# A scale chunk of a joint-attention block loaded through another engine's DMA queue

## The chip, the cores and the metric

The kernel runs on 1 core of one Trainium2 chip. The metric is the device time of one execution in microseconds; before the change it is 116.68 us, the median of 3 runs (116.31 to 116.77). A core has TensorE (matmuls, PE in the profile, its weight loads PEld), VectorE (DVE), ScalarE (ACT), GpSimd (POOL) and SyncE (SP). They run their own instruction streams and wait for each other through semaphores. Transfers between the chip's memory (HBM) and the on-chip memory are issued by SyncE, ScalarE or GpSimd, each into a queue of its own (q1, q10 and q0 in the profile), and 16 DMA engines carry them out.

## The reference

One block of a diffusion transformer with two streams, an image of 2 x 256 tokens and a text of 2 x 32 tokens, 1152 channels, all bf16. Each stream is normalized, scaled and shifted by vectors computed from a condition `c`, and projected to q, k and v; the streams attend jointly; each is projected out, gated and added to its input.

```python
mod_i = (_silu(c) @ wmod_img).reshape(B, 6, 1, D)
shi, sci, gai = (mod_i[:, 0].copy(), mod_i[:, 1].copy(), mod_i[:, 2].copy())
hi = _layernorm(x_img, axis=-1) * (1 + sci) + shi
qkvi = hi @ wqkv_img
...
q = jnp.concatenate([qt, qi], axis=1)
scores = jnp.einsum('bqd,bkd->bqk', q, k) * D ** (-0.5)
p = _softmax(scores, axis=-1)
a = jnp.einsum('bqk,bkd->bqd', p, v)
out_i = x_img + gai * (ai @ wo_img)
```

The change concerns `sci`, the scale of the image stream: columns 1152 to 2303 of `wmod_img`.

## The kernel before

The image stream is four tiles of 128 tokens (x tiles 0 to 3), tiles 0 and 1 of the first image, 2 and 3 of the second. The 1152 channels are nine blocks of 128. The order of instructions on each engine is written out by hand: an engine runs its instructions in the order in which the program names them, and a wait holds all that stands behind it on that engine. TensorE therefore works through the first stage in this order (L261 to L333):

- `warm` (L139): matmuls on zeros, 4, then the transpose of `c` for silu (L148), then 11 more; nothing uses their results.
- `mod_scale(0)` (L213): the scale of channel blocks 0 and 1. `mod_cols` (L207) multiplies 18 blocks of `w_sc_i` by silu(c) (L210); ScalarE adds 1 and writes `mod_i` (L221).
- `x_transposes(0)` (L187, L193): the nine blocks of the normalized tile 0, `xn_i`, are turned so that channels lie on partitions; one warming matmul; the same for tile 1.
- `v_block` with chunk 0 (L256, L250): the value projection of tiles 0 and 1 over the channel blocks 0 and 1, eight matmuls of 128x512.
- the transposes of tile 2, `mod_scale(1)`, the value projection of tile 2, and so on through tile 3 and the chunks 1 to 3, and then the query and key projections and the text stream.

ScalarE evacuates the transposes. Blocks 0 and 1 are scaled on the way (`evac_scaled`, L196 to L199), which needs `mod_i`; the others are copied (`evac_low` L202, `evac_high` L205) and scaled later in place (`apply_mod`, L223). Between these copies ScalarE takes the square root for the normalization (`std_of`, L175). VectorE makes the statistics (L168), the reciprocal (L179) and the normalized tile (`out_of`, L180) in the order tile 0, 1, then 2, with the first third of tile 3's statistics ahead of tile 2's normalization.

The scale weight `w_sc_i` and the value weight `w_v_i` are loaded in four chunks each of two channel blocks (the last of three), `KC` in the code. A scale chunk takes 256 columns of all 1152 rows, in pieces of 512 B. A value chunk takes 256 full rows of 1152 columns, in pieces of 2304 B, and an x tile 128 such rows.

All these loads stand on SyncE's queue in the order of L103 to L114: x tile 0, x tile 1, scale chunk 0, x tile 2, value chunk 0, x tile 3, then scale and value chunks in turn, and behind them the weights of the later stages. On ScalarE's queue stand three transfers ahead of ScalarE's first instruction: the condition `c` (L81, 4.5 KB), and two tiny reads (L84) of 16 rows and 2 columns into a tile `first`, one from the scale weight, one from the value weight. Nothing reads `first`.

The transfers issued by SyncE and ScalarE use eight completion semaphores in rotation: the ninth waits, ahead of its issue, for the landing of the first.

Of the kernel before, what the change touches and what calls it, by code (L numbers as in the profile page):

```python
# [14 lines left out]
def kernel(  # L15
# [14 lines left out]
    nc = tc.nc  # L30
    bf = mybir.dt.bfloat16
# [3 lines left out]
    B, NI, D = x_img.shape  # L35
    NT = x_txt.shape[1]
    P = 128
# [19 lines left out]
    small = ctx.enter_context(tc.tile_pool(name="small", bufs=4))  # L57
# [12 lines left out]
    def w_view(src):  # L70
        return src.rearrange("(kt p) n -> p kt n", p=P)
# [7 lines left out]

    c18 = small.tile([B * KT, P], bf, bufs=1)  # L80
    nc.scalar.dma_start(c18[:], c.rearrange("b (kt p) -> (b kt) p", p=P))  # L81
    first = small.tile([16, 2, 2], bf, bufs=1)
    for n, (src, c0) in enumerate(((wmod_img, D), (wqkv_img, 2 * D))):
        nc.scalar.dma_start(first[:, n, :], src[0:P:8, c0:c0 + 2])  # L84
    x_i = act.tile([P, NIT, D], bf)
    x_t = act.tile([P, D], bf)
    xf_full = act.tile([P, 2 * VC + 64], bf)
# [1 line left out]
    w_sc_i = wpool.tile([P, KT, D], bf, tag="w", name="w_sc_i")  # L89
    w_v_i = act.tile([P, KT, D], bf, tag="V", name="w_v_i")  # L90

    def load_x(i):
        nc.sync.dma_start(x_i[:, i, :], xi_t[:, i, :])  # L93

    def load_sc(ch):
        k0, k1 = KC[ch]
        nc.sync.dma_start(w_sc_i[:, :, k0 * P:k1 * P], w_view(wmod_img)[:, :, D + k0 * P:D + k1 * P])

    def load_v(ch):
        k0, k1 = KC[ch]  # L100
        nc.sync.dma_start(w_v_i[:, k0:k1, :], w_view(wqkv_img)[:, k0:k1, 2 * D:3 * D])

    load_x(0)  # L103
    load_x(1)
    load_sc(0)
    load_x(2)
    load_v(0)
    load_x(3)
    for ch in range(1, len(KC)):
        load_sc(ch)  # L110
        if ch < len(KC) - 1:
            load_v(ch)
# [786 lines left out]
```

## Time and profile before

| what | value |
|---|---|
| median of 3 runs | 116.68 us |
| profiled execution, its own time | 116.51 us |
| its span | 114.5 us |
| TensorE busy | 108.8 us (95%) |
| VectorE, ScalarE, GpSimd busy | 75.0, 39.7, 27.6 us |
| read from HBM | 39.36 MB |
| mean rate over the span | 357 GB/s |
| SyncE's queue q1 | 39.64 MB, 90.9% of 16 engines |
| ScalarE's queue q10 | 0.18 MB, 0.6% |

The span is the time from the first to the last instruction that the profile shows; the execution's own time has what lies around it too. TensorE's idle time falls into the first 10 us and the last 3 us. The rates of the first slices are lower than later: of 40 slices of 2.86 us, the first eight moved 81, 315, 346, 355, 372, 383, 398 and 411 GB/s.

In lines of the timeline and the chain, the first number is the start in us from the span's start, the second the length; what stands in square brackets is how long the engine was idle ahead of it and who ended the wait. "SPq" is SyncE's issue of a transfer; the transfer itself goes on after it. In the list of DMA issues the last number is the time from issue to landing.

### The profile page before, as it was taken

Reading aid. Unit: us, or ns where it says so; the run is one execution under the profiler, and the core shown is the slowest. Engines: PE = TensorE matmul, PEld = TensorE weight load, DVE = VectorE, ACT = ScalarE, POOL = GpSimd, SP = SyncE. Lnnn points to the kernel's source line nnn. Section 1 sums busy time; section 2 is a strip of 40 time slices with the busy share of each in tenths; the row PEclk is TensorE's granted clock in tenths of the full one; section 3 lists DMA queues with packets and bytes.
Section 4 is the critical chain, followed back from the end, with each engine's and each line's share of the span. In section 5 each row is a group of like instructions: output and inputs, shape, how many; then the busy total and the mean of one; then the engine's idle time right before and its main releaser. Section 6 shows DMA issues by size and latency. Waiting matters only on the chain.

```text
span 114.5 us, 2919 instructions
## 1 busy us (share of the span) xinstructions
PE 108.8 (95%) x1230; PEld 64.7 (56%) x1230; DVE 75.0 (66%) x150; ACT 39.7 (35%) x93; POOL 27.6 (24%) x60
## 2 busy tenths in 40 slices
PE   5978999999999999999999999999999999999990
PEld 1344564544954444444447658787697566567560
DVE  1698920353399999999999760227656803998770
ACT  2729760342380630730009924025646700001000
POOL 7000103550050000000000051501540560899200
PEclk9999999999999999999999999999999999999999
DMA  3999999999999999999999999999999999962042
GB/s 81 315 346 355 372 383 398 411 412 411 408 407 412 405 416 401 412 412 411 412 411 411 410 405 411 404 389 399 411 408 403 409 410 398 388 273 102 26 163 69
DMA packets 22775, 40.87 MB, mean 357 GB/s; under 512 B 1311, under 2 KB 6571, under 8 KB 22763
## 3 DMA queue, kind: packets, MB, share of 16 engines
q1 hardware_dynamic: 21680, 39.64, 90.9%
q0 software_dynamic: 608, 0.88, 2.1%
q10 hardware_dynamic: 475, 0.18, 0.6%
q8 instruction: 9, 0.15, 0.5%
q14 instruction: 3, 0.02, 0.1%
HBM read 39.36 MB, written 1.34 MB: 356 GB/s over the span
## 4 chain that ended last, share of the span: by engine, by line
PE 87%; DMA 6%; SPq 2%; DVE 1%; issue 0%
PE qkps L486 31%; PE ps L821 16%; PE va L250 11%; DMA x_i<-in_x_img_dram 6%; PE aps L729 5%; PE ps L552 4%; PE sps L585 4%; PE gps L374 3%; PE ops L839 2%; PE ps L350 2%; PE ps L401 2%; PE ps L660 2%; SPq L93 1%; PE mps L210 1%; PE gps L794 1%; PE tp L193 1%
## 5 line engine op out<-in xcount | busy, mean ns | idle before, releaser
L486 PE MATMUL qkps<-hT_i,t 128*128 128x512 bf16 x162 | 35.6, 379 | 0.0
L486 PEld LDWEIGHTS <-t 128*128 128x128 bf16 x162 | 15.6, 98 | 18.3 <-issue 0.2
L448 DVE SCALAR_TENSOR_TENSOR sacc<-w_v_i,mod_img,sacc 128x1152 f32<-128x1152 bf16 x16 | 22.7, 1418 | 0.5
L821 PE MATMUL ps<-t,aT 128*128 128x384 bf16 x99 | 16.4, 326 | 0.0
L250 PE MATMUL va<-w_v_i,hT_i 128*128 128x512 bf16 x63 | 14.6, 379 | 0.5 <-DMA w_v_i<-in_wqkv_img_dram 0.5
L821 PEld LDWEIGHTS <-aT 128*128 128x128 bf16 x117 | 11.0, 98 | 6.8 <-issue 0.5
L827 DVE TENSOR_TENSOR tmp<-ps,gb 128x384 bf16<-128x384 f32 x11 | 6.1, 551 | 6.1 <-DMA gb<-mod_scratch 4.9
L250 PEld LDWEIGHTS <-hT_i 128*128 128x128 bf16 x63 | 5.8, 97 | 7.2 <-ACT hT_i L198 0.8
L805 POOL TENSOR_TENSOR w_og<-t,gb 128x384 bf16<-128x384 bf16 x9 | 8.8, 1006 | 4.5 <-PE ps L821 4.5
L507 POOL TENSOR_SCALAR svn<-svr 128x128 bf16<-128x128 bf16 x1 | 0.3, 298 | 32.8 <-ACT svr L156 32.8
L168 DVE BATCH_NORM_STATS2 stats<-x_i 128x6 f32<-128x384 bf16 x12 | 5.9, 543 | 2.9 <-DMA x_i<-in_x_img_dram 2.9
L436 ACT ACTIVATE qT<-qkps 128x512 bf16<-128x512 f32 x9 | 4.9, 596 | 6.4 <-PE qkps L486 6.4
L452 ACT CAST shi<-sacc 128x1152 bf16<-128x1152 f32 x2 | 2.3, 1152 | 13.7 <-DVE sacc L448 13.7
L142 PE MATMUL wps<-wz 128*128 128x512 bf16 x16 | 5.6, 499 | 1.2 <-DVE wz L127 1.2
L234 POOL TENSOR_SCALAR hT_i<-hT_i,mod_img 128x256 bf16<-128x256 bf16 x5 | 2.5, 510 | 15.9 <-ACT rstd L175 9.2
L742 DVE TENSOR_SCALAR aT<-aps,sv 128x288 bf16<-128x288 f32 (+2 forms) x11 | 4.3, 457 | 1.9 <-PE aps L729 1.9
L552 PEld LDWEIGHTS <-t 128*128 128x128 bf16 x162 | 4.9, 98 | 0.7 <-issue 0.5
L156 DVE CAST kT<-qkps 128x512 bf16<-128x512 f32 x3 | 2.1, 686 | 4.7 <-PE qkps L486 4.7
L552 PE MATMUL ps<-hT_t,t 128*128 128x64 bf16 x162 | 5.0, 193 | 0.0
L828 DVE TENSOR_TENSOR o<-tmp,x_i 128x384 bf16<-128x384 bf16 x11 | 4.7, 428 | 0.4
L744 ACT ACTIVATE aT<-aps,sv 128x288 bf16<-128x288 f32 (+2 forms) x11 | 4.0, 468 | 2.2 <-PE aps L729 2.2
L729 PE MATMUL aps<-pT,v_i 128*128 128x288 bf16 (+2 forms) x44 | 4.8, 264 | 0.0
(166 smaller groups left out, 148.0 us busy)
## 6 DMA issues: line engine op xcount, KB each, us to landing
t<-in_wmod_txt_dram SPq DMA_DIRECT2D x3, 2592.0 KB, 21.9
t<-in_wqkv_img_dram SPq DMA_DIRECT2D x6, 864.0 KB, 13.1
t<-in_wqkv_txt_dram SPq DMA_DIRECT2D x2, 2592.0 KB, 18.4
t<-in_wmod_img_dram SPq DMA_DIRECT2D x3, 864.0 KB, 11.6
w_home<-in_wmod_img_dram SPq DMA_DIRECT2D x1, 2592.0 KB, 14.7
t<-in_wqkv_txt_dram SPq DMA_DIRECT2D x3, 864.0 KB, 14.2
t<-in_wo_img_dram SPq DMA_DIRECT2D x1, 2592.0 KB, 17.8
t<-in_wo_txt_dram SPq DMA_DIRECT2D x3, 864.0 KB, 15.6
```

The source lines that it names most:

```text
L142: nc.tensor.matmul(ps[:], lhsT=wz[:, 0:P], rhs=wz[:], start=True, stop=True)
L168: nc.vector.bn_stats(stats[0:np_, k, :], x_ap[:, k * CH:(k + 1) * CH])
L250: nc.tensor.matmul(ps[:], lhsT=hT_i[:, kt, i * P:(i + 1) * P], rhs=w_v_i[:, kt, half * VW:(half + 1) * VW], start=(kt == 0), stop=(kt == K ...
L436: nc.scalar.mul(out_ap, in_ap, SCALE)
L448: nc.vector.scalar_tensor_tensor(saccs[b][:], w_v_i[:, kt, :], ap, saccs[b][:], op0=ALU.mult, op1=ALU.add)
L486: nc.tensor.matmul(pss[j - j0][:], lhsT=wq[:, kt, j * P:(j + 1) * P], rhs=hT_i[:, kt, :], start=(kt == 0), stop=(kt == KT - 1))
L552: nc.tensor.matmul(ps[:, j - j0, :], lhsT=wq[:, kt, j * P:(j + 1) * P], rhs=hT_t[:, kt, :], start=(kt == 0), stop=(kt == KT - 1))
L729: nc.tensor.matmul(bank[:, off:off + c1 - c0], lhsT=lhsT, rhs=rhs, start=(first[id(bank)] == n), stop=(final[id(bank)] == n))
L805: nc.gpsimd.tensor_mul(w_og[:, dt, 0:CH], w_o_i[:, dt, NG0:D], gb[:, B - 1, NG0:D])
L821: nc.tensor.matmul(ps[:, 0:cw], lhsT=aT[:, dt, t0:t0 + P], rhs=rhs, start=(dt == DTS[0]), stop=(dt == DTS[-1]))
L827: nc.vector.tensor_mul(tmp[:, 0:cw], ps[:, 0:cw], gb[:, b, cs])
L828: nc.vector.tensor_add(o[:, cs], tmp[:, 0:cw], x_i[:, i, cs])
```

## The change

Scale chunk 0 is issued by ScalarE, behind `c` and the remaining tiny read of the value weight, and no longer by SyncE between x tiles 1 and 2. The tiny read of the scale weight is left out. The other scale chunks stay on SyncE's queue. No computation changes.

```diff
     c18 = small.tile([B * KT, P], bf, bufs=1)
     nc.scalar.dma_start(c18[:], c.rearrange("b (kt p) -> (b kt) p", p=P))
-    first = small.tile([16, 2, 2], bf, bufs=1)
-    for n, (src, c0) in enumerate(((wmod_img, D), (wqkv_img, 2 * D))):
-        nc.scalar.dma_start(first[:, n, :], src[0:P:8, c0:c0 + 2])
+    first = small.tile([16, 2], bf, bufs=1)
+    nc.scalar.dma_start(first[:], wqkv_img[0:P:8, 2 * D:2 * D + 2])
...
-    def load_sc(ch):
+    def load_sc(ch, queue=nc.sync):
         k0, k1 = KC[ch]
-        nc.sync.dma_start(w_sc_i[:, :, k0 * P:k1 * P], w_view(wmod_img)[:, :, D + k0 * P:D + k1 * P])
+        queue.dma_start(w_sc_i[:, :, k0 * P:k1 * P], w_view(wmod_img)[:, :, D + k0 * P:D + k1 * P])
...
+    load_sc(0, nc.scalar)
     load_x(0)
     load_x(1)
-    load_sc(0)
     load_x(2)
     load_v(0)
     load_x(3)
```

## The prediction

> **What bounds the kernel now.** I read the chain that ended last, in order of time, then the timeline of the first 25 us, then the DMA issues and queues of short stretches, last two tables by stretch. The chain (start, length, what):
>
> ```profile
> 2.99 0.43 SPq L101
> 3.42 0.04 issue
> 3.47 6.89 DMA x_i<-in_x_img_dram
> 10.36 0.02 issue
> 10.38 0.56 DVE stats L168
> ...
> 11.68 0.68 PE tp L193 x9
> ...
> 22.18 4.48 PE va L250 x20
> ```
>
> From 11.68 us TensorE runs almost without a break to 111.36 us, through stages that the change does not touch. What delays TensorE at 11.68 is therefore paid at the end, less the small waits before 22 us. The timeline shows what stands ahead of that point:
>
> ```profile
> 7.21 0.58 DVE L180 TENSOR_SCALAR xn_i<-x_i,mv,rstd 128x1152 bf16<-128x1152 bf16 x1
> ...
> 7.30 0.61 PE L210 MATMUL mps<-sT,w_sc_i 128*128 128x2 bf16 x18 [0.79 <-DMA w_sc_i<-in_wmod_img_dram]
> ...
> 8.58 0.67 PE L193 MATMUL tp<-ident,xn_i 128*128 128x128 bf16 x9
> ...
> 9.72 1.89 PE L250 MATMUL va<-w_v_i,hT_i 128*128 128x512 bf16 x8 [0.48 <-DMA w_v_i<-in_wqkv_img_dram]
> ...
> 10.17 0.29 ACT L175 ACTIVATE rstd<-mv,eps_t 128x1 f32<-128x1 f32 x1
> ...
> 20.06 0.91 PEld L210 LDWEIGHTS <-w_sc_i 128*128 128x128 bf16 x27 [0.15 <-DMA w_sc_i<-in_wmod_img_dram]
> ```
>
> TensorE waits for the first scale chunk until 7.30. The normalized tile 0 is ready at 7.21 + 0.58 = 7.79, and the transposes behind the scale matmuls start at 7.85. A chunk that came earlier could win 0.05 us there; one that comes later holds everything behind it on TensorE.
>
> **What a later chunk costs.** Call M the start of the scale matmuls, 7.30 now. The second set of transposes ends at 8.58 + 0.67 = 9.25, that is M + 1.95, and only then can the first value matmuls (L250) run; now they wait 0.48 more for the value weights. Eight of them take 1.89: M + 3.84. Beside them ScalarE makes rstd of x tile 2 behind evacuations that need the chunk, done at 10.46 = M + 3.16; VectorE adds a reciprocal (0.15) and the normalization (0.58), M + 3.89, and the third transposes follow some 0.05 later, M + 3.94. They start at 11.68 now. Of a shift there, the 0.15 us wait at 20.06 gives back 0.15. So the time changes by **M + 3.94 - 11.68 - 0.15 = M - 7.89**. Up to M = 7.89 that is nothing: a chunk 0.59 us later only eats the 0.48 us wait for the value weights, VectorE's wait for x tile 3 (landed at 10.36) and the 0.15 us.
>
> **The change, part by part.** *ScalarE's queue.* The transfer of 0.1 KB that goes took 0.33 us to issue, the chunk 0.43 on SyncE: ScalarE is free at 2.3 in place of 2.2. Its table loads, silu and second table load follow, the last ending at 5.0 against 5.58, when rstd of tile 0 needs it: 0 on the path, with 0.5 of cover. SyncE's slowest early issue of a small transfer, 0.82 (L93 at 2.12), would use 0.4 of that cover; its blocked one, 2.76 (L101 at 4.64), would make tile 0 late by about 0.7, still ahead of a late chunk. I take 0.
>
> *SyncE's queue.* The chunk's issue and the gap behind it, 0.43 + 0.04, go; x tile 2, value chunk 0 and x tile 3 are each issued 0.47 us sooner. They land 6.1, 6.7 and 6.9 us after their issue, and the DMA engines are at a share of 1.02 to 1.16 in every half microsecond from 3.0 to 6.0: they queue for the engines, not for the issue. Worth between 0 and 0.47; I take 0. SyncE also waits 0.2 us at 4.4 for the tiny transfer (waits of SyncE's queue); the next issue is blocked until 7.40 anyway, so 0.
>
> *No tiny read of the scale weight.* No row prices what it does for the chunk. Low 0. High, by the stretch where the engines were slowest once running, 239 GB/s over 5.5 to 6.5 against 302 before it: 63 KB, 0.2 us. I take 0.
>
> *The chunk itself, 576 KB in rows of 512 B.* This decides. In order on one queue it followed x tiles 0 and 1. These are the landings:
>
> ```profile
> w_sc_i<-in_wmod_img_dram SPq DMA_DIRECT2D x1, 576.0 KB, 5.6
> ...
> x_i<-in_x_img_dram SPq DMA_DIRECT2D x1, 288.0 KB, 6.1
> first<-in_wqkv_img_dram ACTq DMA_DIRECT2D x1, 0.1 KB, 4.4
> ...
> w_v_i<-in_wqkv_img_dram SPq DMA_DIRECT2D x1, 576.0 KB, 6.7
> ```
>
> With the issues at 1.65, 2.12, 1.76 and 2.99 they land at 7.25, 8.2, 6.2 and 9.7. After the change the chunk is issued behind c and the other tiny transfer, about 1.76, still at its old time; but SyncE issues x tile 2 at 1.65 and value chunk 0 at about 2.1. It now shares the engines with transfers that used to follow it. How are two queues shared? The queue rows of 94 to 96 us, GpSimd's beside SyncE's:
>
> ```profile
> q0 software_dynamic: 133, 0.54, 65.5%
> q1 hardware_dynamic: 134, 0.30, 38.2%
> ```
>
> 133 packets against 134, though the one kind carries 4 KB and the other 2.2: a turn each by packets, not by bytes. The chunk is 9 x 128 = 1152 packets of 512 B, the x tiles and value chunk 128 to 256 of 2304 B, so turn by turn it loses. Against it stands the 0.1 KB transfer: alone on ScalarE's queue, it landed 4.4 us after its issue, 1.1 us before the chunk that was issued ahead of it on the other queue, where c, on an idle chip, was there 2.3 us after its issue. That is nearer to arrival order than to turns. Low end: arrival order, the chunk behind x tile 2 alone, M = 8.2. High end: turns throughout; some 36 packets of SyncE's on each engine (x tile 2, value chunk 0, x tile 3, the rest of tile 1) go first, so half of the chunk is still to come when x tile 3 lands at 10.36, shared with the next 512 B chunk: 2 x 288 KB at 302 GB/s is 1.9 us, M = 12.3. Between them: the first part in arrival order, the rest in turns with value chunk 0. Then x tiles 0 to 2, the chunk and value chunk 0 all go before its last packet, the same bytes that stood before the value chunk's landing now: **M = 9.72**. I take this, since both rows then hold for their part. Below the low end, with the chunk served even before x tile 1, M would be about 6.3, but tile 1 and with it both normalizations would come later: no gain there.
>
> Sum: 9.72 - 7.89 = +1.83 us. On the profiled execution's 116.51 us (span 114.5) that is 118.34; the median of the runs is 0.17 above it: **118.5 us**.
>
> [...]
>
> **Rivals.** *Turns throughout.* For it the 133 to 134, against it the 4.4 us. M between 10.4 and 12.3, say 11.3: +3.4, 120.1 us.
>
> *Arrival order, behind x tile 2 only.* For and against the other way round. M = 8.2: +0.3, 117.0 us.
>
> *Not slower: two queues fill the engines' gap.* In 5.5 to 6.5 us they moved 239 GB/s; if the chunk's packets ran while another queue's first reads were slow, value chunk 0 and x tile 3 would land up to 0.2 us sooner and the chunk by 7.3: 116.68 - 0.3 = 116.4 us. It decides only where M stays under 7.89, which needs the chunk to get ahead of x tile 2, issued 0.1 us before it. "The transfer is hidden anyway" ends here too, at 116.7.
>
> *The clock falls.* Between 6.51 (last warming matmul) and M TensorE would do nothing for 3.2 us. After its last matmul of all, at 111.36, the granted clock fell at about 114, 2.7 us later:
>
> ```profile
> 111.40:114.00 2.60, 0.00 (x0) 0.00 (x0) 0.28 (x1) 0.00 (x0) 0.00 (x0) 1.00 0.26 76
> 114.00:114.40 0.40, 0.00 (x0) 0.00 (x0) 0.00 (x0) 0.00 (x0) 0.00 (x0) 0.55 0.00 0
> ```
>
> At the start matmuls of 512 columns follow at 427 ns until 4.84 and at 216 after, 3.6 us from the first one at 1.23. A second such stretch at half speed costs 1.8 us on top of the forecast: 120.3 us. Against it: the pause may not last long enough. [...]
>
> **Chances.** Forecast 0.40; turns throughout 0.16; arrival order 0.18; not slower 0.13; the clock falls 0.13. A measurement of this kernel can tell about 0.5%, 0.58 us, from no change. The forecast and the two of 120 us are slower by more: 0.69; of arrival order, a landing a little later adds 0.03. Same: 0.15 of arrival order and 0.08 of not slower. Faster: the remaining 0.05. The range runs from 116.6 (0.1 left out below) to 120.3 (0.1 above); the forecast's own, M from 9.1 to 10.4, is 117.9 to 119.2.
>
> **What would show it.** Right: the scale matmuls (L210) start at about 9.7 with some 3 us of waiting for w_sc_i, the value matmuls about 11.7 with no wait for w_v_i, the third transposes at 13.6, and the wait at 20.06 gone. The share rule shows in the packets of ScalarE's queue beside SyncE's between 4 and 9 us. Wrong: scale matmuls at or before 7.9; then the chunk was not held up, and the sum falls to 0 or below. L250 at 427 ns apart after 10 us would be the clock.

## The result

The changed kernel takes 122.08 us, the median of 6 executions (121.22 to 123.88); the kernel before, run beside it, 116.65 us (116.31 to 117.09). The ratio is 1.0448, 95% interval 1.0417 to 1.048: slower by about 5.2 us. (The two medians lie 5.4 us apart; the ratio leaves out the execution of 123.88 us, in which the granted clock was lowest, 0.958.) The profiled execution took 122.23 us with a span of 120.2 us, 5.7 more than before. The change moved some code, so L209 is what L210 was, L192 was L193, L249 was L250.

The chain that ended last, in order of time, now hangs on the chunk itself:

```profile
1.77 9.46 DMA w_sc_i<-in_wmod_img_dram
11.28 0.64 PE mps L209 x18
11.91 0.98 PE tp L192 x9
...
17.70 0.52 PE tp L192 x9
```

The chunk is issued at 1.77, as expected, and landed only after 9.46 us. The DMA issues of short stretches give the others (x tile 2, the chunk, value chunk 0, x tile 3):

```profile
x_i<-in_x_img_dram SPq DMA_DIRECT2D x1, 288.0 KB, 4.5
...
w_sc_i<-in_wmod_img_dram ACTq DMA_DIRECT2D x1, 576.0 KB, 9.5
...
w_v_i<-in_wqkv_img_dram SPq DMA_DIRECT2D x1, 576.0 KB, 7.5
...
x_i<-in_x_img_dram SPq DMA_DIRECT2D x1, 288.0 KB, 7.9
```

With the issues at 1.64, 1.77, 2.12 and 2.60, x tile 2 landed at 6.1, value chunk 0 at 9.6 and x tile 3 at 10.5: all ahead of the chunk. The last two are no earlier than before. In the timeline:

```profile
3.17 4.60 PE L141 MATMUL wps<-wz 128*128 128x512 bf16 x11
...
7.15 0.58 DVE L179 TENSOR_SCALAR xn_i<-x_i,mv,rstd 128x1152 bf16<-128x1152 bf16 x1
...
11.28 0.64 PE L209 MATMUL mps<-sT,w_sc_i 128*128 128x2 bf16 x18 [3.51 <-DMA w_sc_i<-in_wmod_img_dram]
...
13.12 1.17 PE L192 MATMUL tp<-ident,xn_i 128*128 128x128 bf16 x9
...
14.93 2.77 PE L249 MATMUL va<-w_v_i,hT_i 128*128 128x512 bf16 x6 [0.22 <-ACT hT_i L197]
...
17.49 0.72 PE L192 MATMUL tp<-ident,xn_i 128*128 128x128 bf16 x9
```

The normalization is where it was (7.15 against 7.21) and waits. M, the start of the scale matmuls, is 11.28 in place of 7.30. But the third transposes do not follow at M + 3.94 = 15.22; they start at 17.49, 2.27 us later still. Nine transposes take 1.17 where they took 0.67, and six value matmuls 2.77 where eight took 1.89. The latter start 0.43 us apart, the sign that the prediction had named for a fallen clock. The table by stretches (busy times of PE, PEld, DVE, ACT, POOL, then granted clock, DMA share, GB/s) says why:

```profile
7.50:10.70 3.20, 0.27 (x2) 0.00 (x0) 2.65 (x8) 0.00 (x0) 0.00 (x0) 1.00 1.06 339
10.80:14.10 3.30, 2.82 (x38) 2.55 (x39) 0.32 (x1) 0.80 (x3) 0.00 (x0) 0.50 1.11 376
14.20:17.50 3.30, 3.08 (x9) 1.09 (x9) 1.91 (x5) 2.53 (x7) 0.00 (x0) 0.50 1.07 384
17.60:26.00 8.40, 8.35 (x84) 4.84 (x84) 2.07 (x9) 3.44 (x11) 1.47 (x3) 1.00 1.05 408
```

TensorE did almost nothing from 7.8 to 11.3, its granted clock fell to half at 10.8 and stayed there to 17.6. The pause was 3.51 us only because the warming matmuls ended late: the clock records of the two traces have it rise from its slow start at 7.36 here and at 4.82 before, so 11 warming matmuls took 4.60 us in place of 3.34 and ended at 7.77 in place of 6.51. Two losses add up: 11.28 - 7.89 = 3.39 us for the late chunk and 2.27 us for the clock, 5.66 of the 5.7 us by which the span grew.

How the two queues shared the engines between 7 and 9 us, SyncE's (q1) and ScalarE's (q10):

```profile
q1 hardware_dynamic: 329, 0.53, 74.1%
q10 hardware_dynamic: 325, 0.17, 27.7%
```

As many packets of one queue as of the other (329 and 325), though most of SyncE's were of 2304 B and the chunk's of 512 B: three quarters of the bytes, 0.53 of 0.70 MB, went to SyncE's queue. Earlier it was not so: from 4.5 to 6.0 us the chunk had 385 packets beside 108 of SyncE's. Equal counts alone would also fit turns of several packets each. But in the single DMA records of this trace the chunk's last seven rows start 0.047 us apart, though each took 0.027: that leaves room for about one row of scale chunk 1 between any two and fits turns of single rows there, though the records don't name the engine that a row went by. This rests on the change's own trace; the experiments ask whether it is the cause, what the clock is worth, and what part order of issue has.

### The profile page after: what moved, and what is told of

It is laid out like the page before. It is cut to its first block, busy times and chain, and to the rows that moved or that the text cites. A ratio compares the mean times of both kernels' runs of the same rounds, so it can differ in the third digit from the quotient of the medians.

```text
span 120.2 us, 2910 instructions
## 1 busy us (share of the span) xinstructions
PE 111.7 (93%) x1222; PEld 66.3 (55%) x1230; DVE 75.2 (63%) x150; ACT 39.6 (33%) x93; POOL 27.7 (23%) x60
## 4 chain that ended last, share of the span: by engine, by line
PE 87%; DMA 8%; ACTq 1%; issue 1%; ACT 1%; DVE 0%
PE qkps L485 29%; PE ps L820 15%; PE va L249 12%; DMA w_sc_i<-in_wmod_img_dram 8%; PE aps L728 4%; PE ps L551 4%; PE sps L584 4%; PE gps L373 3%; PE tp L192 2%; PE ops L838 2%; PE mps L209 2%; PE ps L349 2%; PE ps L400 2%; PE ps L659 2%; PE gps L793 1%; PE sps L597 1%
## 5 line engine op out<-in xcount | busy, mean ns | idle before, releaser
L249 PE MATMUL va<-w_v_i,hT_i 128*128 128x512 bf16 x60 | 15.5, 409 | 0.3 <-ACT hT_i L197 0.2
L249 PEld LDWEIGHTS <-hT_i 128*128 128x128 bf16 x63 | 6.2, 104 | 7.4 <-issue 1.4
L141 PE MATMUL wps<-wz 128*128 128x512 bf16 x16 | 7.1, 609 | 1.2 <-DVE wz L126 1.2
L451 ACT CAST shi<-sacc 128x1152 bf16<-128x1152 f32 x2 | 2.3, 1152 | 13.7 <-DVE sacc L447 13.7
L209 PE MATMUL mps<-sT,w_sc_i 128*128 128x2 bf16 x81 | 2.6, 164 | 3.5 <-DMA w_sc_i<-in_wmod_img_dram 3.5
L209 PEld LDWEIGHTS <-w_sc_i 128*128 128x128 bf16 x81 | 2.5, 98 | 4.6 <-DMA w_sc_i<-in_wmod_img_dram 4.1
L218 DVE TENSOR_SCALAR mod_img<-mps 128x4 f32<-128x4 f32 (+1 forms) x3 | 0.5, 163 | 7.3 <-PE mps L209 7.3
```

Of the source, the lines that this page charges most:

```text
L141: nc.tensor.matmul(ps[:], lhsT=wz[:, 0:P], rhs=wz[:], start=True, stop=True)
L209: nc.tensor.matmul(out_ps[:, j - j0, :], lhsT=wt[:, kt, j * P:(j + 1) * P], rhs=sT[:, kt, :], start=(kt == 0), stop=(kt == KT - 1))
L249: nc.tensor.matmul(ps[:], lhsT=hT_i[:, kt, i * P:(i + 1) * P], rhs=w_v_i[:, kt, half * VW:(half + 1) * VW], start=(kt == 0), stop=(kt == K ...
```

## The experiments

**Is it the neighbour, the missing tiny read, or ScalarE's queue?** Three runs take these apart. The first puts the tiny read back into the changed kernel, the second takes it out of the kernel before.

```diff
-    first = small.tile([16, 2], bf, bufs=1)
-    nc.scalar.dma_start(first[:], wqkv_img[0:P:8, 2 * D:2 * D + 2])
+    first = small.tile([16, 2, 2], bf, bufs=1)
+    for n, (src, c0) in enumerate(((wmod_img, D), (wqkv_img, 2 * D))):
+        nc.scalar.dma_start(first[:, n, :], src[0:P:8, c0:c0 + 2])
```

> The changed kernel with the tiny read of the scale weight put back between c and the chunk on ScalarE's queue. Theory (turns by packet): the chunk lands as late as in the changed kernel, scale matmuls at 11.0 to 11.5 us, time 121 to 123 us. Rival (the chunk is slow because its first reads are no longer prepared by the tiny one): scale matmuls at 9 us or earlier, time 118.5 us or less.

```diff
-    first = small.tile([16, 2, 2], bf, bufs=1)
-    for n, (src, c0) in enumerate(((wmod_img, D), (wqkv_img, 2 * D))):
-        nc.scalar.dma_start(first[:, n, :], src[0:P:8, c0:c0 + 2])
+    first = small.tile([16, 2], bf, bufs=1)
+    nc.scalar.dma_start(first[:], wqkv_img[0:P:8, 2 * D:2 * D + 2])
```

> The kernel before with only the tiny read of the scale weight taken out; the chunk stays on SyncE's queue. Theory (turns by packet): scale matmuls at 7.2 to 7.6 us, time 116.3 to 117.2 us. Rival (missing tiny read): the chunk lands 0.6 us or more later and the time rises by 0.6 us or more.

The changed kernel with the read took 122.44 us (ratio to before 1.0491, 1.0427 to 1.0555), scale matmuls at 11.83, somewhat later than expected; the chunk was issued 0.46 us later there (2.23). The kernel before without it took 116.64 us (0.9978, 0.995 to 1.0007), scale matmuls at 7.26. The tiny read of the scale weight is worth nothing that can be measured, in either place.

The third leaves the chunk on ScalarE's queue, but holds SyncE's queue from x tile 2 on, so that the chunk has no neighbour:

```diff
-    load_x(2)
...
-    stats_of(0, 0, NCH)
+    stats_of(0, 0, 2)
+    nc.vector.memset(x_i[:, 2, 0:1], 0.0)
+    load_x(2)
...
+    stats_of(0, 2, NCH)
```

All of SyncE's loads from x tile 2 on move along with `load_x(2)`.

> The changed kernel, but SyncE's queue from x tile 2 on is held until VectorE has made two thirds of tile 0's statistics (about 4.7 us): VectorE writes one element of x tile 2's place there, and x tile 2's load waits for it. The chunk stays on ScalarE's queue, without the tiny read, but has no neighbour to take turns with. Theory (turns by packet): scale matmuls at 6.9 to 7.6 us; value chunk 0 and x tile 3 land as late as before or up to 0.7 us later; time 116.5 to 117.5 us. Rivals (ScalarE's queue is slow by itself, or the missing tiny read): scale matmuls at 9 us or later, time over 118 us.

It took 118.24 us (1.0104, 1.0036 to 1.0172). The scale matmuls and the first value matmuls in its timeline:

```profile
7.42 0.60 PE L195 MATMUL mps<-sT,w_sc_i 128*128 128x2 bf16 x18 [0.17 <-DMA w_sc_i<-in_wmod_img_dram]
...
11.62 1.89 PE L235 MATMUL va<-w_v_i,hT_i 128*128 128x512 bf16 x8 [2.34 <-DMA w_v_i<-in_wqkv_img_dram]
```

The chunk is back at 7.42, on ScalarE's queue and without the tiny read: the neighbour was the cause. The time was missed by 0.7 us, for a plain reason: x tile 2 was issued only at 4.86, the engines moved only 209 GB/s from 4.0 to 5.5 us, and value chunk 0 landed at 11.6 in place of 9.7. The wait changed its name.

**What is the clock worth?** The changed kernel with 27 warming matmuls in place of 11.

```diff
-    warm(11)
+    warm(27)
```

> The changed kernel with 27 warming matmuls in place of 11 behind the transpose of c, so that TensorE has no pause of 3.5 us ahead of the scale matmuls. Theory (turns by packet delay the chunk, and the granted clock fell because TensorE paused): the scale matmuls (L209) still start at about 11.3 us, the granted clock stays at 1.0 from about 8 us on, the third transposes start at 11.27 + 3.94 = 15.2 us and the time is 116.65 + (11.27 - 7.89) = 120.0 us, 119.5 to 120.6. Rival (the clock cost nothing, the delay behind the chunk is longer than the formula says): the third transposes stay near 17.5 us and the time at 122 us.

120.51 us (1.0317, 1.0263 to 1.0371), 1.6 us less than the changed kernel, at granted clock 1.0 in all four executions and although the chunk came 0.74 us later in the profiled one. In the timeline and the table by stretches:

```profile
12.02 0.60 PE L209 MATMUL mps<-sT,w_sc_i 128*128 128x2 bf16 x18 [1.32 <-DMA w_sc_i<-in_wmod_img_dram]
...
15.90 0.68 PE L192 MATMUL tp<-ident,xn_i 128*128 128x128 bf16 x9 [0.31 <-DVE xn_i L179]
```

```profile
6.30:9.60 3.30, 3.30 (x17) 1.47 (x15) 3.16 (x10) 0.29 (x1) 0.00 (x0) 1.00 1.04 362
9.70:13.00 3.30, 1.98 (x33) 1.25 (x32) 0.65 (x2) 0.18 (x1) 0.00 (x0) 1.00 1.10 371
```

The chunk landed even later in this execution, M = 12.02, and yet the third transposes start at 15.90, M + 3.88: with the clock held, the forecast's sum from M to the third transposes is right within 0.06 us. The span is 118.8, 4.3 above before, where M - 7.89 gives 4.1. So both losses are real and separate. The run with the tiny read shows the clock's loss at about half its size, with 3.41 us at half clock in place of 6.83:

```profile
8.20:11.50 3.30, 0.00 (x0) 0.00 (x0) 2.21 (x6) 0.00 (x0) 0.00 (x0) 1.00 1.12 349
11.60:14.90 3.30, 3.07 (x38) 2.68 (x39) 0.00 (x0) 0.93 (x4) 0.00 (x0) 0.50 1.09 376
15.00:18.00 3.00, 2.85 (x36) 1.70 (x34) 1.94 (x6) 2.82 (x9) 0.00 (x0) 1.00 1.07 380
```

Its third transposes start at 16.82, 1.05 us behind M + 3.94. In the clock records of its trace 6.83 us at full clock are followed by 3.41 at half, in those of the changed kernel 3.41 at full by 6.83 at half.

**By packets or by bytes?** The chunk as two transfers of one channel block each: twice as many packets, half the size, the same bytes.

```diff
-    load_sc(0, nc.scalar)
+    for j in range(2):
+        nc.scalar.dma_start(w_sc_i[:, :, j * P:(j + 1) * P], w_view(wmod_img)[:, :, D + j * P:D + (j + 1) * P])
```

> The changed kernel with the chunk issued as two transfers on ScalarE's queue, of one channel block each: twice as many packets of half the size, 256 B, the same bytes. Theory (one packet each in turn): 144 packets on each engine need 144 turns; they are through only after x tile 2, value chunk 0, x tile 3, scale chunk 1 and value chunk 1, so the last scale matmuls of the chunk start at 13.5 to 15.5 us and the time is over 124 us. Rival (the queues share by bytes, or the chunk is late for its place alone): scale matmuls end at 11 to 12.3 us, time 121 to 123 us.

122.71 us (1.05, 1.0405 to 1.0595; two executions), scale matmuls in two parts, and the queues between 8.5 and 10 us, when SyncE's was sending scale chunk 1:

```profile
10.04 0.38 PE L210 MATMUL mps<-sT,w_sc_i 128*128 128x2 bf16 x9 [2.48 <-DMA w_sc_i<-in_wmod_img_dram]
...
13.79 0.40 PE L210 MATMUL mps<-sT,w_sc_i 128*128 128x2 bf16 x9 [3.38 <-DMA w_sc_i<-in_wmod_img_dram]
```

```profile
q1 hardware_dynamic: 616, 0.31, 69.6%
q10 hardware_dynamic: 613, 0.16, 45.8%
```

616 packets, all but two of 512 B, against 613, all but three of 256 B: in this stretch the queues shared by packets, and the second half came at 13.8 as expected. The first half came earlier than by turns alone. The time stayed 1.3 us under what was expected and falls into the rival's range; it is the packet counts and the scale matmuls, which end at 14.2 and not by 12.3, that exclude sharing by bytes.

**Turns from the first packet on?** Four runs change the order or the moment of issue. In the mirror of the change, value chunk 0 with its large packets goes to ScalarE's queue in the kernel before.

```diff
...
+    load_v(0, nc.scalar)
     load_x(0)
     load_x(1)
     load_sc(0)
     load_x(2)
-    load_v(0)
```

> The mirror of the change on the kernel before: the first scale chunk stays on SyncE's queue between x tiles 1 and 2, both tiny reads stay, and value chunk 0 goes to ScalarE's queue behind them. Its packets are 256 of 2304 B against the chunk's 1152 of 512 B. Theory (one packet each in turn): now the large packets win; value chunk 0 is there by 6.5 to 7.3 us instead of 9.7, the scale chunk is later by about the value chunk's own transfer, scale matmuls at 8.0 to 9.0 us, x tile 2 lands at about 9.7; time 117 to 118 us. Rival (order of arrival): scale matmuls at 7.2 to 7.5, value chunk 0 behind the scale chunk at 8 us or later, time within 0.6 us of before. Rival (ScalarE's queue is served last whatever it carries): value chunk 0 lands at 9.5 us or later.

118.76 us (1.0182, 1.0112 to 1.0252), above what was expected. Scale matmuls at 9.27, a little later than expected, and x tile 2 at 9.8. But value chunk 0, issued at 2.23, landed at 10.3, and this falls against turns from the first packet. Queues from 4 to 5.5 us, then from 6.5 to 8.5:

```profile
q1 hardware_dynamic: 728, 0.37, 88.9%
q10 hardware_dynamic: 21, 0.00, 0.8%
```

```profile
q10 hardware_dynamic: 182, 0.39, 52.2%
q1 hardware_dynamic: 282, 0.37, 51.3%
```

From 4 to 5.5 us the value chunk sent nothing (21 packets, 0.00 MB): it stood behind the scale chunk, issued 0.6 us sooner on the other queue. Then the two shared, though not one for one (182 to 282). So order of issue counted over both queues here. That turns begin where both have packets waiting is my reading, which fits this; why a transfer waits for one issued sooner on the other queue, no run shows. The rival "ScalarE's queue is last whatever it carries" would fit this landing too; the run with the chunk in front, below, excludes it. A shorter hold of SyncE's queue, to about 3 us:

```diff
     for b in range(B):
         nc.gpsimd.memset(ones32[:, b, b:b + 1], 1.0)
+    nc.gpsimd.memset(x_i[:, 2, 0:1], 0.0)
...
+    load_x(2)
```

As in the longer hold, all of SyncE's loads from x tile 2 on move along.

> The changed kernel with SyncE's queue held from x tile 2 on until GpSimd has made its first constants (about 3.0 us; GpSimd writes one element of x tile 2's place). Theory (one packet each in turn): a dose between the changed kernel (no hold, scale matmuls 11.3) and the hold to 4.8 us (7.4): some 15 to 20 of the chunk's 72 packets on each engine go alone, the others share; scale matmuls at 9 to 10.5 us, time 118.5 to 121 us. Rival (the delay comes in one step, from standing behind x tile 2): 11.3 or 7.4.

Two executions of 118.28 and 120.95 us. Scale matmuls at 8.75, between 11.28 without a hold and 7.42 with the long one, though earlier than expected. From 4 to 5.5 us:

```profile
q10 hardware_dynamic: 686, 0.35, 82.0%
q1 hardware_dynamic: 4, 0.00, 0.8%
```

The same 1.5 us in the changed kernel had 258 packets of ScalarE's queue beside 139 of SyncE's. What went before the neighbour came was spared the sharing.

The chunk ahead of the tiny read of the value weight, and the chunk as ScalarE's very first issue. The first edit is shown; the second moves the two lines of `c` down as well:

```diff
-    first = small.tile([16, 2], bf, bufs=1)
-    nc.scalar.dma_start(first[:], wqkv_img[0:P:8, 2 * D:2 * D + 2])
...
     load_sc(0, nc.scalar)
+    first = small.tile([16, 2], bf, bufs=1)
+    nc.scalar.dma_start(first[:], wqkv_img[0:P:8, 2 * D:2 * D + 2])
```

> The changed kernel with the chunk and the tiny read of the value weight swapped on ScalarE's queue: the chunk is issued at about 1.4 us, ahead of x tile 2 (1.65), where the changed kernel issues it at 1.77 behind it. Theory (packets come to the engines in the order of issue over both queues, and take turns one by one only once both have packets waiting): x tile 2 and value chunk 0 arrive behind it, more of the chunk goes alone, scale matmuls at 7.8 to 10 us, time 117 to 120 us. Rival (turns from the first packet on, whatever the order of issue): scale matmuls within 0.6 us of 11.3, time 121 to 123 us.

> The changed kernel with the chunk as ScalarE's first issue, at about 0.75 us, ahead of c and the tiny read. Theory (order of issue first, then turns): only x tile 0 is as early; the chunk shares turns with x tile 1 and x tile 2, is nearly through before value chunk 0 comes, scale matmuls at 6.5 to 8.3 us; c and x tile 1 land up to 1 us later; time 116.4 to 118 us. Rival (turns from the first packet on): 32 packets of SyncE's and part of scale chunk 1 still go first, scale matmuls at 10 us or later, time over 119.5 us.

The swap gave 121.28, 121.75 and 122.53 us, and once 117.07 at granted clock 1.0. The profiled execution has scale matmuls at 10.82, later than the theory had it and where the rival put them; three of the four times are in the rival's range too. Its trace says otherwise for most of the chunk: from 4 to 5.5 us it sent 511 packets, against 258 in the changed kernel, and of its 16 completions eleven were in by 7.0 us. The other five came from 7.6 to 10.8, and the scale matmuls started behind the last. What held these five is not shown, as the records don't name the engine that a packet went by; whether the fourth execution was spared it is open, as it has no trace. The run does not decide between theory and rival by its times.

With the chunk in front the order of issue shows most, with 874 packets of the chunk's queue against 15 of SyncE's. Queues from 3 to 4.5 us, then the chunk and x tile 1 in the DMA issues:

```profile
q10 hardware_dynamic: 874, 0.45, 99.8%
q1 hardware_dynamic: 15, 0.03, 4.8%
```

```profile
w_sc_i<-in_wmod_img_dram ACTq DMA_DIRECT2D x1, 576.0 KB, 5.4
...
x_i<-in_x_img_dram SPq DMA_DIRECT2D x1, 288.0 KB, 4.8
```

Issued at 0.74 it landed at 6.2, on ScalarE's queue; x tile 1, issued at 1.18 on SyncE's, stood behind most of it and landed at 6.0; value chunk 0 landed at 8.4 and x tile 3 at 9.2, 1.2 us sooner than before. The time was missed all the same: 119.92 us (1.0293, 1.0232 to 1.0354). The condition c stood behind the chunk too, landed at 6.2, and TensorE's 11 warming matmuls stand behind its transpose; they took 4.81 us, as they followed 0.43 us apart to the last in this execution, so the scale matmuls began at 11.06, with the chunk there for 4.9 us. What I had expected as "c and x tile 1 land up to 1 us later" was over 3 us for c.

**Is there a version that beats both?** Two tries with all 15 warming matmuls ahead of the transpose of c: the last kernel, and the kernel before with c behind x tile 1 on SyncE's queue and no tiny reads.

```diff
-    warm(4)
+    warm(15)
     silu_c()
-    warm(11)
```

> The kernel with the chunk as ScalarE's first issue, and all 15 warming matmuls ahead of the transpose of c, so that they don't wait for c, which lands at about 6.2 us there. Theory (the chunk is early, the late c and the warming behind it made that run slow): chunk landed by 6.5 us, scale matmuls at 7 to 8.2 us, tile 0 normalized at 8.5 to 9.2 (ScalarE's table load and rstd stand behind the silu of the late c), time 116.8 to 118.2 us. Rival (two queues cost the time whatever the order): time 119 us or more.

> A try at a kernel better than both: the kernel before, all loads on SyncE's one queue in its old order, but c behind x tile 1 on that queue, both tiny reads left out, ScalarE's queue empty, and all 15 warming matmuls ahead of the transpose of c. In the run with the chunk as ScalarE's first issue all landings came within 0.5 us on the 16 engines and value chunk 0 landed at 8.4 us instead of 9.7. Theory (the small reads at the very front put some engines behind): landings close together, value chunk 0 at 8.4 to 9.2 us, scale matmuls at 7.0 to 7.8, time 116.0 to 116.4 us. Rival (they cost nothing, the order of the big transfers made that): value chunk 0 at 9.3 to 10 us, time 116.4 to 117.2 us.

With the chunk in front: 119.3 us (1.0259, 1.0208 to 1.0309), as the rival had it; 117.73 in the profiled execution, as the theory had it, at granted clock 1.0, where the other three had 0.970 to 0.985. Scale matmuls at 7.12, chunk landed at 6.4, value chunk 0 at 8.5; then

```profile
8.90 0.58 DVE L179 TENSOR_SCALAR xn_i<-x_i,mv,rstd 128x1152 bf16<-128x1152 bf16 x1
...
9.54 0.68 PE L192 MATMUL tp<-ident,xn_i 128*128 128x128 bf16 x9 [1.83 <-DVE xn_i L179]
```

The late c, transposed at 6.66, holds ScalarE's table load (7.08 to 8.36) and with it tile 0's rstd (8.38). The other try took 117.34 us (1.0062, 1.0028 to 1.0097). Its xn_i came at 8.48, for a different reason: the transpose of c, at 6.24, waited for no transfer there but stood behind the 15 warming matmuls (1.23 to 6.30). Value chunk 0 was issued 1.03 us later than before (4.02) and landed at 10.5, its 16 completions spread over 2.3 us: taking the small reads from the front did not bring the landings closer together. Five of its 12 executions had a granted clock of 0.985, near the 0.986 of the run with the tiny read, and took 118.3 to 118.9 us, the other seven 116.6 to 117.4. Neither beats the kernel before.

## Why the prediction was wrong in size

**Right.** That the stage before 11.7 us decides and is paid in full; that a later chunk costs M - 7.89 (within 0.2 us in the run with 27 warming matmuls); that ScalarE's later start, SyncE's earlier issues and the missing tiny read are worth nothing (ScalarE's second table load ends at 5.02 against 5.00, value chunk 0 was issued 0.87 us sooner and landed at 9.6 against 9.7, and without the tiny read the ratio is 0.9978); that the queues shared by packets and not by bytes, from 7 to 9 us (329 to 325); and the direction.

**Wrong: the value taken for M.** The step "Then x tiles 0 to 2, the chunk and value chunk 0 all go before its last packet", which gave M = 9.72, let the chunk's tail take turns with value chunk 0 alone. Its form was right, a first part in order of issue and then turns, but the tail was mis-sized: it also took turns with x tile 3 and scale chunk 1, which SyncE issues without a pause (2.60, 3.11), and beside its packets of 512 B went as many of SyncE's, 206 of the 329 from 7 to 9 us of 2304 B. By the DMA records, all of x tile 3 and over 900 of scale chunk 1's 1152 rows had started before the chunk's last one. M was 11.28, between the forecast and the high end of 12.3. That is 1.56 us of the 3.83 by which the profiled execution's two losses, 5.66 us, exceed the forecast's 1.83. The "turns throughout" rival named M = 11.3, but as the middle of 10.4 to 12.3, and by turns from the first packet on; the 385 packets against 108 speak against that. That it met 11.28 is in part luck.

**Wrong: the clock as an alternative.** The fall was listed as a rival that adds 1.8 us to the forecast. The step that failed is "Against it: the pause may not last long enough", with a chance of 0.13 of its own. The fall is no alternative to a late chunk, since waiting for the chunk is what makes the pause: all six executions of the changed kernel show a lowered clock (0.958 to 0.971), after a pause of 3.51 us in the profiled one, not far from the 3.2 us of the forecast's own M. It comes on top of the delay, and it cost 2.27 us, the rest of the 3.83, since the clock stayed at half for 6.83 us and not for the 3.6 that the rival had taken from the start of the trace. The sum of both rivals, 120.1 + 1.8 = 121.9 us, comes near 122.08, with a size too small for the clock; the range ended at 120.3 because two rivals that go together were counted side by side.

What the traces show of the sharing are equal counts, 329 to 325 and 616 to 613, starts 0.047 us apart where the chunk's last rows can be told apart, and a part in order of issue ahead of them (385 to 108).

## What to carry to other kernels

A load that decides when a stage starts should not be put on a second queue beside larger packets without asking what it will share with: here from 7 to 9 us the queues went one packet for one (329 to 325), so the chunk in rows of 512 B got a quarter of the bytes, and the last of its 16 completions decided (the first at 6.8 us, the last at 11.2). The order of one queue is a tool, worth 3.4 us here ahead of what the clock added. Before pricing a wait on TensorE, ask what its length does to the clock: here a pause of 3.5 us added two thirds of the delay's own cost, 2.27 us to 3.39.

## What the runs showed of the hardware that was not expected

- A transfer issued on one queue stood behind one issued sooner on the other: with the chunk in front x tile 1 of 288 KB, issued at 1.18, landed at 6.0 behind the chunk issued at 0.74; before the change it landed at 4.4.
- From 7 to 9 us in the changed kernel and from 8.5 to 10 us in the run with packets of 256 B, the packets of the two queues went one for one at different sizes (329 to 325, 616 to 613); in the mirror run, from 6.5 to 8.5 us, they did not (182 to 282).
- The granted clock also fell where TensorE had not been idle: with the short hold it was at half from 9.36 us on, after 3.40 us in which TensorE was busy for 1.72 (1.1 of it warming matmuls of 512 columns, the rest matmuls of 2 columns and transposes), and in the run with the tiny read it stayed at 1.00 after 3.40 us with 1.75, all warming matmuls. The line of the latter stands last:

```profile
5.95:9.35 3.40, 1.72 (x26) 0.90 (x25) 3.29 (x10) 0.29 (x1) 0.00 (x0) 1.00 1.03 349
9.36:12.70 3.34, 3.12 (x21) 2.23 (x21) 1.24 (x3) 1.94 (x8) 0.00 (x0) 0.50 1.10 375
...
4.70:8.10 3.40, 1.75 (x8) 0.59 (x6) 3.25 (x11) 1.38 (x3) 0.00 (x0) 1.00 0.92 308
```

The next stretch of that run, from 8.20, is in the table above. What the clock goes by, no run shows.
- With the chunk in front the 16 completions of value chunk 0 came within 0.53 us of each other (7.87 to 8.40) and x tile 3 behind it landed 1.2 us sooner; in the kernel before the spread is 1.38 us (8.30 to 9.68). With no small read ahead of x tiles 0 and 1 it was 2.3 us, so such reads alone are not the reason; what is stays open.
